# Routed attention with a squared-ReLU feed-forward on one core: the feed-forward of the last two batches by Strassen's algorithm after all attention, that of the first two spread evenly

## The chip, the cores and the metric

The kernel runs on one core of a Trainium2 chip. The metric is device time in microseconds (us) for one execution; the kernel before has a median of 1128.75 us over 3 runs (1128.17 to 1129.24). The profiler names the engines: PE (matrix products; PEld is its loading of the stationary operand), DVE (vector), ACT (scalar, activations), POOL (GpSimd), SP (issues the DMAs).

## What is computed

Four batches (b) of 768 tokens, eight heads of 64. Each query and key is assigned to the nearest of 16 centroids of its head; attention is masked to pairs of one cluster. The heads side by side form x (3072 x 512), which goes through a feed-forward:

```python
scores = scale * np.matmul(q, k.transpose(0, 1, 3, 2))
scores = np.where(mask, scores, -1000000000.0)
attn = softmax(scores)            # over keys
x = concat_heads(attn @ v)        # (3072, 512)
h = x @ w_in                      # w_in: 512 x 2048
g = np.maximum(h, 0) ** 2
out = g @ w_out                   # w_out: 2048 x 512
```

All of it is float32.

## The kernel before

**Attention.** Two heads (a pair) are worked on at once; there are 16 pairs, four for each batch. A pair has two query halves h of 384 tokens, and each half is done in three units, each over two chunks of 128 keys: 96 units. A unit on PE is a group of score products into `sc` (line 81 and 84, by `together`), ACT takes the exponential of 128x1536 (line 360), DVE multiplies by the mask in four instructions (line 366, from batch 1 on; batch 0 has its mask in the score products), POOL adds the exponentials up in `acc` (lines 376 and 378), and two units later PE multiplies by v into `av`. When a half of a pair is through, `finish` sums `acc` over the keys on PE (`sm`), DVE takes the reciprocal (line 416), scales `av` into the tile `xT` (line 417) and notes in `good` whether the numbers were in range (line 422).

**Feed-forward.** `ffn(b, h)` treats one half of a batch's tokens, 384 of them: 16 times four matmuls of 384 columns into `ph` (line 435), ReLU on ACT and squaring on DVE (`gT`, line 443); then for three blocks of 128 tokens 16 matmuls of 512 columns into `po` (line 448), an ACT copy and a DMA out. One half is 64 + 48 = 112 matmuls. A float32 matmul shows in the trace as two passes, each a MATMUL with a LDWEIGHTS of its own, so a half has 128 passes of 384 columns and 96 of 512.

**Order of the work.** `ffn` is a generator that yields after each matmul. The main loop over units calls `fill_steps` twice per unit, and so puts feed-forward matmuls between the attention products. Before the change the share per unit is what is left of the appended halves over the units until the next ones come: the two halves of batch b run beside the attention of batch b+1, and both halves of batch 3 run after all attention. Each engine works its own queue in order; the recording layer can move an instruction by priority, so the built order is shown below where it matters. After the last unit a check is made: `fine` sums `good` on DVE, PE adds it over the partitions (`every`, line 554), DVE makes `flag` (line 555). If it is set, `general_path` recomputes everything; it is not taken here.

**Weights** come in by DMA in the first 15 or so units and are rounded by ACT, DVE and POOL (lines 139 to 155).

Of the kernel before, what the change touches and what calls it, by code (L numbers as in the profile page):

```python
# [8 lines left out]
F32 = mybir.dt.float32  # L9
# [15 lines left out]
def kernel(  # L25
# [10 lines left out]
    nc = tc.nc  # L36

    B, H, S, D = q.shape
    C = centroids.shape[1]
    NCH = S // P  # L40
    DM = H * D
    DFF = moe_w_in.shape[1]
    KT = DM // P
    FT = DFF // P
    HP = H // 2
    NB = NCH // 2
    TB = NB * P
# [2 lines left out]
    SCALE = float(D) ** -0.5  # L50

    const = ctx.enter_context(tc.tile_pool(name="const", bufs=1))
    outer, ctx = ctx, ExitStack()
    loads = ctx.enter_context(tc.tile_pool(name="loads", bufs=4))
    loads_v = ctx.enter_context(tc.tile_pool(name="loads_v", bufs=2))
    qktp = ctx.enter_context(tc.tile_pool(name="qktp", bufs=HP))
# [3 lines left out]
    expp = ctx.enter_context(tc.tile_pool(name="expp", bufs=3))  # L60
    accp = ctx.enter_context(tc.tile_pool(name="accp", bufs=2))
    rbp = ctx.enter_context(tc.tile_pool(name="rbp", bufs=2))
    xtp = ctx.enter_context(tc.tile_pool(name="xtp", bufs=2))
    gtp = ctx.enter_context(tc.tile_pool(name="gtp", bufs=FT))

    early = ExitStack()
    wstage = early.enter_context(tc.tile_pool(name="wstage", bufs=AHEAD, side="right"))
    once_early = early.enter_context(tc.tile_pool(name="once_early", bufs=1, side="right"))
    later = {}
# [263 lines left out]
    def first_half(pair, h):  # L333
        return pair < HP and h == 0

    av = {}
    xT = {}
# [61 lines left out]
    def finish(pair, h):  # L399
        b, hp = divmod(pair, HP)  # L400
        if hp == 0:
            pool = xtp if (2 * b + h) % 3 < 2 else later["xT"]
            xT[b, h] = pool.tile([P, KT, TB], F32, name="xT")
        if first_half(pair, h):
            sm = sums.pop((pair, h))
        else:
            total = acc.pop((pair, h))
            sm = bank("sm", [P, TB])
            together(
                dict(  # L410
                    out=sm[D * e : D * (e + 1)], lhsT=ups, rhs=total[:, e], start=True, stop=True
                )
                for e in range(2)
            )
# [12 lines left out]

    out_view = out.rearrange("(b p j) m -> b j p m", p=P, j=NCH)

    def ffn(b, h):  # L430
        gT = []
        for f in range(FT):
            ph = bank("ph", [P, TB])
            for kk in range(KT):
                nc.tensor.matmul(  # L435
                    ph, lhsT=w_in[:, kk, f * P : (f + 1) * P], rhs=xT[b, h][:, kk],
                    start=(kk == 0), stop=(kk == KT - 1),
                )
                if kk < KT - 1:
                    yield  # L440
            gT.append(gtp.tile([P, TB], F32, name="gT"))
            nc.scalar.activation(out=gT[f], in_=ph, func=ACT.Relu)  # L442
            nc.vector.tensor_tensor(out=gT[f], in0=gT[f], in1=gT[f], op=ALU.mult)  # L443
            yield
        for i in range(NB):
            po = bank("po", [P, DM])
            for f in range(FT):
                nc.tensor.matmul(  # L448
                    po, lhsT=gT[f][:, i * P : (i + 1) * P], rhs=w_out[:, f],
                    start=(f == 0), stop=(f == FT - 1),  # L450
                )
                if f < FT - 1:
                    yield
            osb = later["out"].tile([P, DM], F32, name="osb")
            nc.scalar.copy(out=osb, in_=po)  # L455
            nc.sync.dma_start(out_view[b, h * NB + i], osb)
            yield

    units = [
        (pair, h, c)
        for pairs, halves in [(range(HP), [0]), (range(HP), [1])]
# [2 lines left out]
    ]  # L466
    LAG = 2
    per_half = FT * KT + NB * FT
    fill = []
    left = [0]  # L470

    def fill_steps(n):
        while n > 0 and fill:
            if next(fill[0], "end") == "end":
                fill.pop(0)
            else:
                n -= 1
                left[0] -= 1

    def next_pair(u):  # L480

        pair, h, c = units[u]
        if c == 0 and pair + 1 < NG and h == 0 and (pair + 1) not in qkT:
            if pair + 1 < HP or pair >= HP:
                return pair + 1
        if c == 0 and h == 1 and pair == HP - 1:
            return pair + 1
        return None
# [5 lines left out]
        item()  # L494
    load_v(0)
    ahead = []
    left_units = [0]
    for _ in range(AHEAD):
        load_weights(next(loaded))
    for u in range(len(units) + LAG):  # L500
        if u < len(units):
            pair, h, c = units[u]
            if (p := next_pair(u)) is not None:
                ahead.extend(prep(p))
            if c == 0 and u + 3 < len(units) and units[u + 3][0] not in raw_v:
                load_v(units[u + 3][0])
            scores(pair, h, c)
        done = None
        if u >= LAG:
            pair, h, c = units[u - LAG]  # L510
            times_v(pair, h, c)
            if c == NCH - 2:
                done = pair, h

        for _ in range(2):
            i = next(to_round, None)
            if i is not None:
                round_weights(i)
                if (i := next(loaded, None)) is not None:
                    load_weights(i)  # L520
            elif not later:
                early.close()
                for name, bufs in (("xT", 1), ("out", 2)):
                    later[name] = ctx.enter_context(
                        tc.tile_pool(name=name + "_late", bufs=bufs, side="right",
                                     reuse_waits="tile")
                    )
        share = -(-left[0] // max(1, left_units[0]))
        left_units[0] -= 1
        fill_steps(share // 2)  # L530
        for _ in range(3):
            if ahead:
                ahead.pop(0)()
        fill_steps(share - share // 2)
        if done:
            pair, h = done
            finish(pair, h)
            b, hp = divmod(pair, HP)
            if h == 1:
                for d in (qkT, ids, qid):  # L540
                    d.pop(pair)
            if h == 1 or b == 0:
                raw_v.pop(pair)
            if hp == HP - 1 and (h == 1 or b == 0):
                for hh in [h] if b == 0 else range(2):
                    fill.append(ffn(b, hh))
                    left[0] += per_half
                left_units[0] = NCH * HP // 2 if b == 0 and h == 0 else NCH * HP

    flag = const.tile([P, 1], I32, name="flag")  # L550
    fine = small.tile([P, 1], F32, name="fine")
# [3 lines left out]
    nc.vector.tensor_scalar(  # L555
        out=flag[0:1], in0=every, scalar1=UP * float(P * 2 * NG * TB), scalar2=None, op0=ALU.is_lt
    )
    for g in fill:
        for _ in g:
            pass  # L560

    ctx.close()
    again = nc.values_load(flag[0:1, 0:1], min_val=0, max_val=1)
    with tc.If(again != 0):
        general_path(
# [187 lines left out]
```

## Time and profile before

| | |
|---|---|
| median of 3 runs | 1128.75 us |
| profiled execution, its time | 1127.61 us |
| its span, first to last instruction | 1125.7 us |
| PE busy | 1084.8 us, 96% |
| DVE, POOL, ACT busy | 574.4, 318.6, 305.9 us |
| last attention product starts | 947.87 us |
| last feed-forward matmuls | 952.9 to 1119.9 us |

A matmul's end is modelled and overlaps the next one's start, so a pace is read from the distance between starts or from a long uninterrupted run, not from the length of one record.

### The profile page before, as it was taken

To read this page: it belongs to the slowest core of one execution; us is meant where nothing else is said; L and a number is where in the kernel's file an instruction comes from. 1 tells how busy PE (TensorE), PEld (TensorE's weight loads), DVE (VectorE), ACT (ScalarE), POOL (GpSimd) and SP (SyncE) were. 2 spreads that over 40 slices of the span, in tenths; PEclk is the share of its full clock that TensorE was granted. 3 is DMA by queue.
4 is the path that set the end of the run, shared out by engine and by line. 5 is a ranking of instruction groups with operands and counts; after the bars stand their busy time and mean duration, and the time that the engine had idled before them with its cause. 6 is when DMAs were issued, how large, how long until landed. Compare 5 with 4: busy or idle time off the path is not lost.

```text
span 1125.7 us, 10447 instructions
## 1 busy us (share of the span) xinstructions
PE 1084.8 (96%) x4195; PEld 503.9 (45%) x4195; DVE 574.4 (51%) x762; ACT 305.9 (27%) x416; POOL 318.6 (28%) x181
## 2 busy tenths in 40 slices
PE   5779999999999999999999999999999998999997
PEld 3333454444444344444445444444445443544543
DVE  4999222328886666672377544664466641200200
ACT  4666322223332223231232212231132210110100
POOL 2444433225443443331333222332232330000000
PEclk8899999999999999999999999999999999999999
DMA  8874000120110201010201002000000000000000
GB/s 226 224 236 152 15 15 14 52 61 1 43 43 1 52 10 52 1 43 9 52 10 42 1 9 61 1 15 10 10 24 0 1 10 19 1 10 19 1 10 21
DMA packets 63880, 44.30 MB, mean 39 GB/s; under 512 B 51536, under 2 KB 56656, under 8 KB 63824
## 3 DMA queue, kind: packets, MB, share of 16 engines
q1 hardware_dynamic: 63824, 43.56, 13.5%
q8 instruction: 35, 0.57, 0.2%
q14 instruction: 21, 0.17, 0.1%
HBM read 37.26 MB, written 6.29 MB: 39 GB/s over the span
## 4 chain that ended last, share of the span: by engine, by line
PE 86%; DVE 7%; issue 3%; DMA 1%; ACT 1%; POOL 1%; SPq 1%; ACTq 0%; POOLq 0%; DVEq 0%
PE po L448 30%; PE ph L435 29%; PE sc L81 6%; PE av L81 5%; PE sc L84 5%; PE av L84 5%; DVE ex L366 2%; PE sm L81 2%; PE pt L237 2%; DVE w_raw L151 1%; DMA w_raw<-in_moe_w_in_dram 1%; DVE rb L416 1%; PE lg L81 1%; PE pb L315 1%; POOL w_out L155 1%
## 5 line engine op out<-in xcount | busy, mean ns | idle before, releaser
L435 PE MATMUL ph<-xT,w_in 128*128 128x384 f32 x1024 | 352.7, 495 | 0.1
L448 PE MATMUL po<-w_out,gT 128*128 128x512 f32 x768 | 347.3, 599 | 0.0
L378 POOL TENSOR_TENSOR acc<-acc,ex 128x768 f32<-128x768 f32 x112 | 219.5, 1959 | 416.8 <-DVE ex L366 358.7
L366 DVE SCALAR_TENSOR_TENSOR ex<-qid,ids,ex 128x384 f32<-128x384 bf16 x288 | 246.2, 916 | 154.9 <-ACT ex L360 151.8
L435 PEld LDWEIGHTS ph<-xT,w_in 128*128 128x128 f32 x1024 | 188.6, 190 | 152.8 <-issue 33.4
L448 PEld LDWEIGHTS po<-w_out,gT 128*128 128x128 f32 x768 | 139.9, 190 | 173.1 <-issue 170.6
L360 ACT ACTIVATE ex<-sc 128x1536 f32<-128x1536 f32 x96 | 139.2, 1450 | 231.8 <-PE sc L84 231.8
L443 DVE TENSOR_TENSOR gT<-gT 128x384 f32<-128x384 f32 x128 | 95.5, 751 | 194.6 <-ACT gT L442 194.2
L84 PE MATMUL sc<-qkT 64*128 64x384 f32 x576 | 151.8, 506 | 0.0
L84 PE MATMUL av<-ex,v_raw 128*64 128x384 f32 x576 | 147.7, 498 | 0.0
L442 ACT ACTIVATE gT<-ph 128x384 f32<-128x384 f32 x128 | 62.9, 492 | 260.9 <-PE ph L435 260.9
L416 DVE RECIPROCAL rb<-sm 128x384 f32<-128x384 f32 x32 | 81.7, 2553 | 67.2 <-PE sm L84 67.1
L81 PE MATMUL sc<-qkT 64*128 64x384 f32 x192 | 89.2, 545 | 1.7 <-ACT ex L360 1.5
L376 POOL TENSOR_TENSOR acc<-ex 128x768 f32<-128x768 f32 x28 | 52.7, 1881 | 123.7 <-DVE ex L366 103.0
L81 PE MATMUL av<-ex,v_raw 128*64 128x384 f32 x192 | 83.1, 515 | 0.0
L84 PEld LDWEIGHTS sc<-qkT 64*128 64x128 f32 x576 | 66.7, 190 | 26.2 <-issue 2.1
L84 PEld LDWEIGHTS av<-ex,v_raw 128*64 128x64 f32 x576 | 46.6, 137 | 35.4 <-issue 35.1
L455 ACT COPY osb<-po 128x512 f32<-128x512 f32 x24 | 14.1, 586 | 175.7 <-PE po L448 175.7
L81 PEld LDWEIGHTS sc<-qkT 64*128 64x128 f32 x192 | 29.0, 189 | 50.3 <-issue 40.0
L81 PEld LDWEIGHTS av<-ex,v_raw 128*64 128x64 f32 x192 | 18.6, 135 | 44.0 <-issue 43.1
L151 DVE SCALAR_TENSOR_TENSOR w_raw<-w_raw 128x512 uint32<-128x512 uint32 x32 | 36.2, 1130 | 0.1
L155 POOL TENSOR_TENSOR w_in<-w_in,w_raw 128x512 int32<-128x512 int32 x16 | 21.7, 1358 | 43.6 <-DVE w_raw L151 38.5
(80 smaller groups left out, 500.8 us busy)
## 6 DMA issues: line engine op xcount, KB each, us to landing
w_raw<-in_moe_w_in_dram SPq DMA_DIRECT2D x16, 512.0 KB, 5.4
w_raw<-in_moe_w_out_dram SPq DMA_DIRECT2D x16, 512.0 KB, 3.5
v_raw<-in_v_dram SPq DMA_DIRECT2D x20, 384.0 KB, 3.3
q_raw<-in_q_dram SPq DMA_DIRECT2D x32, 192.0 KB, 3.5
k_raw<-in_k_dram SPq DMA_DIRECT2D x32, 192.0 KB, 3.9
out_dram<-osb SPq DMA_DIRECT2D x24, 256.0 KB, 2.0
cen<-in_centroids_dram SPq DMA_DIRECT2D x1, 32.0 KB, 1.8
```

The source lines that it names most:

```text
L81: nc.tensor.matmul(**next(products))
L84: nc.tensor.matmul(**product)
L151: nc.vector.scalar_tensor_tensor(out=lo, in0=hi, scalar=0x80000000, in1=lo, op0=ALU.bitwise_and, op1=ALU.bitwise_or)
L360: nc.scalar.activation(out=t, in_=sc.rearrange("p i e n -> p (i e) n")[:, :, 0:TB], func=ACT.Exp, scale=SCALE)
L366: nc.vector.scalar_tensor_tensor(out=to, in0=qid[pair][1][:, h, e], scalar=ids[pair][:, ch % NB, 2 + ch // NB, e : e + 1], in1=to, op0=ALU ...
L376: nc.gpsimd.tensor_tensor(out=acc[pair, h], in0=t[:, 0:2], in1=t[:, 2:4], op=ALU.add)
L378: nc.gpsimd.tensor_tensor(out=acc[pair, h], in0=acc[pair, h], in1=t[:, 2 * i : 2 * i + 2], op=ALU.add)
L416: nc.vector.reciprocal(out=rb, in_=sm)
L435: nc.tensor.matmul(ph, lhsT=w_in[:, kk, f * P : (f + 1) * P], rhs=xT[b, h][:, kk], start=(kk == 0), stop=(kk == KT - 1),)
L442: nc.scalar.activation(out=gT[f], in_=ph, func=ACT.Relu)
L443: nc.vector.tensor_tensor(out=gT[f], in0=gT[f], in1=gT[f], op=ALU.mult)
L448: nc.tensor.matmul(po, lhsT=gT[f][:, i * P : (i + 1) * P], rhs=w_out[:, f], start=(f == 0), stop=(f == FT - 1),)
```

## The change

The first two batches keep `ffn`: four halves (`PLAIN`), 448 matmuls, whose share per unit is now all that is left over all units that are left. Batches 2 and 3 are no longer filled in. When attention and the filling are done, `ctx.close()` gives its memory back and `ffn_pair` runs for batch 2 and then for batch 3, both halves of the batch at once.

`ffn_pair` multiplies by Strassen's algorithm in Winograd's form, one level: operands are cut into 2 x 2 blocks, seven products of blocks replace eight, and sums and differences of blocks are made before and after. First layer: x is cut by contraction (two of four 128-blocks) and by half h; w_in by contraction and by columns. For each of 8 pairs of column blocks there are 7 products of 2 matmuls of 384 columns. POOL makes four combinations of w_in blocks for each (`w_s1` to `w_s4`, 128x256), DVE four of x per batch (`x_t1`, `x_t2`, `x_t4`, and one in place, 128x768). Second layer: for each of 3 token blocks 7 products of 8 matmuls of 256 columns; POOL makes four combinations of w_out once (`w_t1` to `w_t4`, 128x2048), DVE four of g per token block (128x1024). `combine` takes the first product out of PSUM by an ACT copy and adds the others by seven DVE instructions. ReLU and squaring of one block in four are done by ACT, of the others by one DVE instruction each. The tile pool of PSUM banks has 8 buffers here.

```diff
-    outer, ctx = ctx, ExitStack()
+    outer, ctx, keep, early = ctx, ExitStack(), ExitStack(), ExitStack()
+    xtp = keep.enter_context(tc.tile_pool(name="xtp", bufs=2))
...
-            pool = xtp if (2 * b + h) % 3 < 2 else later["xT"]
+            pool = xtp if (2 * b + h) in (0, 1, 5, 6) else later["xT"]
...
+    def ffn_pair(pools, b):
+        gp, sp, tp, bk = pools
+        H2, F2, M2 = KT // 2, FT // 2, DM // 2
+        x = [[xT[b, h][:, H2 * g : H2 * (g + 1)] for h in range(2)] for g in range(2)]
+        t1, t2, t4 = (tp.tile([P, H2, TB], F32, name=f"x_t{i}") for i in (1, 2, 4))
...
+        sub(t1, x[0][1], x[0][0])
+        sub(t2, x[1][1], t1)
+        sub(t4, t2, x[1][0])
+        sub(x[0][1], x[1][1], x[0][1])
+        t3 = x[0][1]
+        g = gp.tile([P, FT, 2, TB], F32, name="g")
+        def combine(c, product, width):
+            (c11, c12), (c21, c22) = c
+            def add(j, *results):
+                bank = bk(width)
+                product(j, bank)
+                for out, to in results:
+                    nc.vector.tensor_tensor(out=out, in0=bank, in1=to, op=ALU.add)
+            bank = bk(width)
+            product(1, bank)
+            nc.scalar.copy(out=c11, in_=bank)
+            add(6, (c12, c11))
+            add(2, (c11, c11))
+            add(7, (c21, c12))
+            add(5, (c22, c21), (c12, c12))
+            bank = bk(width)
+            product(4, bank)
+            sub(c21, c21, bank)
+            add(3, (c12, c12))
+        for i in range(F2):
...
+            nc.gpsimd.tensor_tensor(out=s1, in0=a[1][0], in1=a[1][1], op=ALU.add)
+            sub(s2, s1, a[0][0], nc.gpsimd)
+            sub(s3, a[0][0], a[1][0], nc.gpsimd)
+            sub(s4, a[0][1], s2, nc.gpsimd)
+            operands = {
+                1: (a[0][0], x[0][0]), 2: (a[0][1], x[1][0]), 3: (s4, x[1][1]), 4: (a[1][1], t4),
+                5: (s1, t1), 6: (s2, t2), 7: (s3, t3),
+            }
...
+            combine(c, product, TB)
+            nc.scalar.activation(out=c[0][0], in_=c[0][0], func=ACT.Relu)
+            nc.scalar.square(c[0][0], c[0][0])
+            for to in (c[1][1], c[1][0], c[0][1]):
+                nc.vector.scalar_tensor_tensor(
+                    out=to, in0=to, scalar=0.0, in1=to, op0=ALU.max, op1=ALU.mult
+                )
+        for i in range(NB):
...
+            nc.vector.tensor_tensor(out=s1, in0=a[1][0], in1=a[1][1], op=ALU.add)
+            sub(s2, s1, a[0][0])
+            sub(a[1][0], a[0][0], a[1][0])
+            operands = {
+                1: (a[0][0], w_q[0][0]), 2: (a[0][1], w_q[1][0]), 3: (a[0][1], w_q[1][1]),
+                4: (a[1][1], w_t[4]), 5: (s1, w_t[1]), 6: (s2, w_t[2]), 7: (a[1][0], w_t[3]),
+            }
...
+            combine(c, product, M2)
+            for h in range(2):
+                nc.sync.dma_start(out_view[b, h * NB + i], osb[h])
...
+    PLAIN = [(0, 0), (0, 1), (1, 0), (1, 1)]
-    left = [0]
+    left = [len(PLAIN) * per_half]
...
-        share = -(-left[0] // max(1, left_units[0]))
+        share = -(-left[0] // (len(units) + LAG - u))
...
-    for g in fill:
-        for _ in g:
-            pass
+    fill_steps(left[0])
     ctx.close()
+    fast = ExitStack()
+    banks = fast.enter_context(tc.tile_pool(name="banks", bufs=8, space=PSUM))
...
+    for to, x, y in ((1, w_q[0][1], w_q[0][0]), (2, w_q[1][1], w_t[1]), (3, w_q[1][1], w_q[0][1]),
+                     (4, w_t[2], w_q[1][0])):
+        nc.gpsimd.tensor_tensor(out=w_t[to], in0=x, in1=y, op=ALU.subtract)
+    for b in range(B):
+        if (b, 0) not in PLAIN:
+            ffn_pair(pools, b)
```

Lines of the changed program are one higher than before up to the new functions.

PE's queue at the end of attention, before the change (`av`, `sm`: the last half of the last pair; `every`: the check):

```order
L448 MATMUL po<-w_out,gT 128x512 x9
L81 MATMUL av<-ex,v_raw 64x384
L84 MATMUL av<-ex,v_raw 64x384 x3
L448 MATMUL po<-w_out,gT 128x512 x9
L81 MATMUL sm<-acc,ups 64x384
L84 MATMUL sm<-acc,ups 64x384
L554 MATMUL every<-ups,fine 1x1
L435 MATMUL ph<-xT,w_in 128x384 x64
L448 MATMUL po<-w_out,gT 128x512 x48
```

The same place after the change (`bank`: a product of Strassen's algorithm; the numbers at `x_t` and `w_s` tell buffers apart, 4248 is `w_s2`, 4240 `x_t2`):

```order
L449 MATMUL po<-w_out,gT 128x512 x5
L82 MATMUL av<-ex,v_raw 64x384
L85 MATMUL av<-ex,v_raw 64x384 x3
L449 MATMUL po<-w_out,gT 128x512 x5
L82 MATMUL sm<-acc,ups 64x384
L85 MATMUL sm<-acc,ups 64x384
L650 MATMUL every<-ups,fine 1x1
L516 MATMUL bank<-xT,w_in 128x384 x2
L516 MATMUL bank<-x_t_4240,w_s_4248 128x384 x2
L516 MATMUL bank<-xT,w_in 128x384 x2
```

Between the last groups of `av` five matmuls of the filling stand in place of nine, and behind `every` PE meets as its second product one that needs a sum of POOL and a difference of DVE.

POOL's queue at that place, after the change (4231, 4233, 4232, 4234 are `w_t1`, `w_t3`, `w_t2`, `w_t4`; 4247 to 4250 are `w_s1` to `w_s4` of the first step). Before the change nothing but the check of `flag` follows the last `acc`:

```order
L379 TENSOR_TENSOR acc<-acc,ex 128x768 x4
L672 TENSOR_TENSOR w_t_4231<-w_out 128x2048
L672 TENSOR_TENSOR w_t_4233<-w_out 128x2048
L672 TENSOR_TENSOR w_t_4232<-w_out,w_t_4231 128x2048
L672 TENSOR_TENSOR w_t_4234<-w_t_4232,w_out 128x2048
L505 TENSOR_TENSOR w_s_4247<-w_in 128x256
L470 TENSOR_TENSOR w_s_4249<-w_in 128x256
L470 TENSOR_TENSOR w_s_4248<-w_s_4247,w_in 128x256
L470 TENSOR_TENSOR w_s_4250<-w_in,w_s_4248 128x256
```

The combinations of w_out, which only the second layer needs, stand ahead of those of w_in, which PE's second product needs. `w_t3` waits for the last `av` product, whose `v_raw` lay in its memory.

DVE's queue at the same place, after the change (`x_t1`, `x_t2`, `x_t4` of batch 2; the `xT` difference is the one in place):

```order
L470 TENSOR_TENSOR x_t1_4239<-xT_2683,xT_2535 128x768
L417 RECIPROCAL rb_4192<-sm_4189 128x384
L470 TENSOR_TENSOR x_t2_4240<-xT_2683,x_t1_4239 128x768
L418 SCALAR_TENSOR_TENSOR xT_3635<-av_4158,rb_4192 128x384
L423 SCALAR_TENSOR_TENSOR ok_4195,good_135<-rb_4192 128x384
L470 TENSOR_TENSOR x_t4_4241<-x_t2_4240,xT_2535 128x768
L648 TENSOR_REDUCE fine_4198<-good_135 128x1
L470 TENSOR_TENSOR xT_2683<-xT_2683 128x768
L651 TENSOR_SCALAR flag_4197<-every_4200 1x1
```

Before the change only the reciprocal, the scaling, `ok`, `fine` and `flag` stand there. The first product waits for `flag`, whose PSUM bank it takes over.

DVE's queue between the two layers of batch 2, after the change (4570 and 4574 are the banks of the last two products, `x_t*_48..` belong to batch 3, `g_s1` and `g_s2` to the second layer):

```order
L470 TENSOR_TENSOR g_4246<-g_4246,bank_4570 128x384
L470 TENSOR_TENSOR x_t1_4826<-xT_3635,xT_3493 128x768
L487 TENSOR_TENSOR g_4246<-bank_4574,g_4246 128x384
L526 SCALAR_TENSOR_TENSOR g_4246<-g_4246 128x384 x2
L470 TENSOR_TENSOR x_t2_4827<-xT_3635,x_t1_4826 128x768
L534 TENSOR_TENSOR g_s1_4583<-g_4246 128x1024
L470 TENSOR_TENSOR x_t4_4828<-x_t2_4827,xT_3493 128x768
L470 TENSOR_TENSOR g_s2_4584<-g_s1_4583,g_4246 128x1024
```

The second product of the second layer needs `g_s2`; three differences for batch 3 stand among the instructions that lead to it.

## Rows read from the trace of the kernel before

**Rows 1.** The page's first part: busy us, share of the span, instructions.

```profile
PE 1084.8 (96%) x4195; PEld 503.9 (45%) x4195; DVE 574.4 (51%) x762; ACT 305.9 (27%) x416; POOL 318.6 (28%) x181
```

**Rows 2.** Windows: stretch, us, busy (count) of each engine, granted clock, DMA.

```profile
111.00:947.80 836.80, 832.68 (x3278) 379.94 (x3276) 457.81 (x572) 219.47 (x282) 274.81 (x142) 1.00 0.08 22
947.80:952.90 5.10, 1.06 (x8) 0.33 (x7) 3.77 (x5) 0.59 (x1) 0.00 (x0) 1.00 0.14 51
952.90:1120.00 167.10, 166.91 (x450) 85.77 (x448) 18.02 (x33) 18.79 (x38) 0.00 (x0) 0.99 0.02 9
```

**Rows 3.** Chain that ended last, its tail: start, us, engine, tile, line, passes.

```profile
952.96 43.17 PE ph L435 x128
996.13 41.20 PE po L448 x96
1037.33 41.28 PE ph L435 x128
1078.61 41.21 PE po L448 x96
```

**Rows 4.** Timeline: one weight load among the 512-column passes; four transposes of 128 columns.

```profile
1118.36 0.19 PEld L448 LDWEIGHTS po<-w_out,gT 128*128 128x128 f32 x1 [0.24 <-issue]
...
741.94 0.42 PEld L237 LDWEIGHTS pt<-ident,q_raw 128*128 128x128 f32 x4 [0.55 <-ACT gT L442]
```

**Rows 5.** Windows of one stretch, of lines 435, 448 and 360 alone.

```profile
257.40:416.10 158.70, 44.13 (x122) 21.61 (x122) 1.00 0.10 26
...
257.40:416.10 158.70, 38.20 (x80) 13.90 (x80) 1.00 0.10 26
...
257.40:416.10 158.70, 30.48 (x21) 1.00 0.10 26
```

**Rows 6.** Timeline of the end of attention.

```profile
947.87 0.54 PE L81 MATMUL sm<-acc,ups 128*64 128x384 f32 x1
...
948.78 2.56 DVE L416 RECIPROCAL rb<-sm 128x384 f32<-128x384 f32 x1 [23.08 <-PE sm L84]
951.37 0.56 DVE L417 SCALAR_TENSOR_TENSOR xT<-av,rb 128x384 f32<-128x384 f32 x1
951.85 0.55 DVE L422 SCALAR_TENSOR_TENSOR ok<-rb 128x384 bf16<-128x384 f32 x1
...
952.77 0.19 PE L554 MATMUL every<-ups,fine 128*1 128x1 f32 x2 [4.04 <-DVE fine L552]
...
952.89 12.28 PE L435 MATMUL ph<-xT,w_in 128*128 128x384 f32 x32
```

**Rows 7.** Timeline of POOL and DVE side by side.

```profile
383.88 1.81 POOL L378 TENSOR_TENSOR acc<-acc,ex 128x768 f32<-128x768 f32 x1 [0.56 <-DVE ex L366]
...
384.51 0.56 DVE L272 TENSOR_TENSOR best<-lt,mx 128x384 bf16<-128x384 f32 x1
...
385.10 1.00 DVE L276 TENSOR_TENSOR best<-best,order 128x384 bf16<-128x384 bf16 x1
```

**Rows 8.** Lines 378 and 155: duration ns min/median/max, first and last start.

```profile
L378 POOL TENSOR_TENSOR acc<-acc,ex x112: 1802/2022/2211, 120.8 to 925.8; 128x768 f32<-128x768 f32 x112
...
L155 POOL TENSOR_TENSOR w_in<-w_in,w_raw x16: 1279/1304/1558, 16.7 to 66.9; 128x512 int32<-128x512 int32 x16
```

**Rows 9.** Timeline: two DVE instructions of 512 and 384 elements.

```profile
744.36 0.69 DVE L240 COPY qkT<-pt 128x512 f32<-128x512 f32 x1 [1.05 <-PE pt L237]
...
745.53 0.56 DVE L443 TENSOR_TENSOR gT<-gT 128x384 f32<-128x384 f32 x1 [0.48 <-ACT gT L442]
```

**Rows 10.** The page's fifth part: the mask multiply.

```profile
L366 DVE SCALAR_TENSOR_TENSOR ex<-qid,ids,ex 128x384 f32<-128x384 bf16 x288 | 246.2, 916 | 154.9 <-ACT ex L360 151.8
```

**Rows 11.** Timeline of the end of the span.

```profile
1119.89 0.59 ACT L455 COPY osb<-po 128x512 f32<-128x512 f32 x1 [13.15 <-PE po L448]
1120.50 0.33 SPq L456 DMA_DIRECT2D out_dram<-osb  x1
```

More of the change, by code (lines that the diff above doesn't have):

```diff
@@ L62 @@
     rbp = ctx.enter_context(tc.tile_pool(name="rbp", bufs=2))
-    xtp = ctx.enter_context(tc.tile_pool(name="xtp", bufs=2))
     gtp = ctx.enter_context(tc.tile_pool(name="gtp", bufs=FT))
-    early = ExitStack()
     wstage = early.enter_context(tc.tile_pool(name="wstage", bufs=AHEAD, side="right"))
@@ L457, in ffn, with sub, product @@
             yield
+    def ffn_pair(pools, b):
[3 more added lines that the diff above has]
+        t1, t2, t4 = (tp.tile([P, H2, TB], F32, name=f"x_t{i}") for i in (1, 2, 4))
+        def sub(out, a, b, eng=nc.vector):
+            eng.tensor_tensor(out=out, in0=a, in1=b, op=ALU.subtract)
+        sub(t1, x[0][1], x[0][0])
[23 more added lines that the diff above has]
+        for i in range(F2):
+            lo, hi = slice(i * P, (i + 1) * P), slice((F2 + i) * P, (F2 + i + 1) * P)
+            a = [[w_in[:, H2 * g2 : H2 * (g2 + 1), cols] for g2 in range(2)] for cols in (lo, hi)]
+            s1, s2, s3, s4 = (sp.tile([P, H2, P], F32, name=f"w_s{j}") for j in range(1, 5))
+            nc.gpsimd.tensor_tensor(out=s1, in0=a[1][0], in1=a[1][1], op=ALU.add)
[6 more added lines that the diff above has]
+            }
+            def product(j, bank):
+                for kk in range(H2):
+                    nc.tensor.matmul(
+                        bank, lhsT=operands[j][0][:, kk], rhs=operands[j][1][:, kk],
+                        start=(kk == 0), stop=(kk == H2 - 1),
+                    )
+            c = [[g[:, f, h] for h in range(2)] for f in (i, F2 + i)]
+            combine(c, product, TB)
[4 more added lines that the diff above has]
+                    out=to, in0=to, scalar=0.0, in1=to, op0=ALU.max, op1=ALU.mult
+                )
+        for i in range(NB):
+            cols = slice(i * P, (i + 1) * P)
+            a = [[g[:, F2 * g2 : F2 * (g2 + 1), h, cols] for g2 in range(2)] for h in range(2)]
+            s1, s2 = (sp.tile([P, F2, P], F32, name=f"g_s{j}") for j in (1, 2))
+            nc.vector.tensor_tensor(out=s1, in0=a[1][0], in1=a[1][1], op=ALU.add)
[5 more added lines that the diff above has]
+            }
+            def product(j, bank):
+                for f in range(F2):
+                    nc.tensor.matmul(
+                        bank, lhsT=operands[j][0][:, f], rhs=operands[j][1][:, f],
+                        start=(f == 0), stop=(f == F2 - 1),
+                    )
+                if j == 2:
+                    sub(a[0][1], a[0][1], s2)
+            osb = [later["out"].tile([P, DM], F32, name="osb") for _ in range(2)]
+            c = [[osb[h][:, M2 * m : M2 * (m + 1)] for m in range(2)] for h in range(2)]
+            combine(c, product, M2)
+            for h in range(2):
+                nc.sync.dma_start(out_view[b, h * NB + i], osb[h])
@@ L496 @@
     ahead = []
-    left_units = [0]
     for _ in range(AHEAD):
@@ L522 @@
                 early.close()
-                for name, bufs in (("xT", 1), ("out", 2)):
-                    later[name] = ctx.enter_context(
+                for name, bufs in (("xT", 3), ("out", 2)):
+                    later[name] = keep.enter_context(
                         tc.tile_pool(name=name + "_late", bufs=bufs, side="right",
@@ L527 @@
                     )
-        share = -(-left[0] // max(1, left_units[0]))
-        left_units[0] -= 1
+        share = -(-left[0] // (len(units) + LAG - u))
         fill_steps(share // 2)
@@ L544 @@
             if hp == HP - 1 and (h == 1 or b == 0):
[L545 to L548, printed above, removed]
+                for half in [(b, h)] if b == 0 else [(b, 0), (b, 1)]:
+                    if half in PLAIN:
+                        fill.append(ffn(*half))
     flag = const.tile([P, 1], I32, name="flag")
@@ L557 @@
     )
-    for g in fill:
-        for _ in g:
-            pass
+    fill_steps(left[0])
     ctx.close()
+    fast = ExitStack()
+    banks = fast.enter_context(tc.tile_pool(name="banks", bufs=8, space=PSUM))
+    wtp = fast.enter_context(tc.tile_pool(name="wtp", bufs=1, reuse_waits="tile"))
+    pools = [
+        fast.enter_context(tc.tile_pool(name=name, bufs=1, reuse_waits="tile"))
+        for name in ("gp", "sp", "tp")
+    ] + [lambda width: banks.tile([P, width], F32, name="bank", tag="bank")]
+    w_q = [
+        [w_out[:, FT // 2 * g : FT // 2 * (g + 1), DM // 2 * m : DM // 2 * (m + 1)] for m in range(2)]
+        for g in range(2)
+    ]
+    w_t = {i: wtp.tile([P, FT // 2, DM // 2], F32, name=f"w_t{i}") for i in range(1, 5)}
+    for to, x, y in ((1, w_q[0][1], w_q[0][0]), (2, w_q[1][1], w_t[1]), (3, w_q[1][1], w_q[0][1]),
[4 more added lines that the diff above has]
+            ffn_pair(pools, b)
+    fast.close()
+    keep.close()
     again = nc.values_load(flag[0:1, 0:1], min_val=0, max_val=1)
```

## Prediction

> **What bounds the kernel now.** I read the page's busy line first: PE is busy 96% of the span, every other engine about half or less [rows 1]. An average hides stages, so next the windows. From 111 us to the end of attention PE is busy 832.7 of 836.8 us at granted clock 1.00; then comes a hole of 5 us, and 167 us of feed-forward alone in which PE is again full and POOL idle [rows 2]. So PE sets the end nearly everywhere, and a matmul pass taken away is worth its own pace. The tail of the chain gives that pace without any modelled ends: 128 passes of 384 columns take 41.28 us, 0.3225 each, and 96 passes of 512 columns 41.21 us, 0.4293 each [rows 3]. The first run of 384 columns, behind the hole, took 1.9 us more; the mean clock of that stretch is 0.99. What the hole consists of I read from the timeline: from `sm` at 947.87 DVE needs the reciprocal, scaling, `ok` and `fine` before PE may do `every`, and `ph` starts at 952.89 [rows 6].
>
> **Products saved.** A batch now has 256 passes of 384 and 192 of 512 columns: 82.6 + 82.4 = 165.0 us. Strassen's form has 8 x 7 x 2 matmuls of 384 columns (224 passes) and 3 x 7 x 8 of 256 (336 passes). The trace has no weight-changing float32 pass of 256 columns. Between 384 and 512 the pace is 0.83 ns per column with 2 ns left over, so 256 columns should take 0.2157. Against that stands the weight load, recorded at 0.19 us for each pass [rows 4]: it fits under 0.2157, by little. Four loads of the same size for transposes took 0.42 us together, so they follow each other at 0.105 or less; I take 0.2157. The upper end would be pass and load one after the other, 0.213 + 0.19 = 0.40. With 0.2157: 72.2 + 72.5 = 144.7 us, 20.3 saved for a batch, **40.5 us** for two.
>
> **Attention with less filling.** Two of the six halves that were filled in leave it, 165 us, so `sm` should come at about 783. That holds if a unit still costs the same without its filling. Over 111 to 947.8 it is (836.8 - 495)/85 units = 4.02 us. The stretch with the thinnest filling, 202 passes over 21 units or 4.8 matmuls per unit, gives 158.7 - 122 x 0.3225 - 80 x 0.4293 = 85.0 us, 4.05 per unit [rows 5]. The change puts in 448/85 = 5.3. So the score, exponential, mask, product chain stays hidden; 0.03 us over some 70 units would be 2 us, I add **1**, with 0 and 4 as ends.
>
> **The hand-over.** Here the change adds waits. POOL's new queue has four 2048-element instructions ahead of the first `w_s`. The cheapest 512 and 768 elements took 1.28 and 1.80 us [rows 8], 2.04 ns per element, so 2048 should take 4.4 and 256 should take 0.76; at the median of 768 it would be 5.4. On DVE 384 and 512 elements take 0.56 and 0.69 [rows 9], so 768 take 0.95 and 1024 take 1.21. And the two engines hold each other up: while POOL added from 383.88 to 385.69, a DVE instruction with one operand in PSUM took its 0.56, the next one, with both in SBUF, took 1.00 and ended 0.4 behind POOL [rows 7]. The differences `x_t`, `ok` and the in-place one have both operands in SBUF.
>
> Take `sm` as zero. Between the last scores and `sm` PE has 15 matmuls of 512 columns (12.9 us) and four attention groups, some 20 us; POOL's last addition comes some 10 us after those scores (the exponential, 30.48/21 = 1.45 [rows 5], a reciprocal's work ahead of four masks at 0.92 [rows 10], additions of 2.0). So POOL starts `w_t1` at -10, `w_t3` behind the last `av` at -5, `w_t2` ends at 4.1. DVE does the reciprocal until 3.5, `x_t2` is held until 4.1 and ends at 5.1; `w_t4` runs from there to 9.5, the scaling beside it, `ok` is held until it ends: 10.0. `x_t4` takes turns with `w_s1` to 11.7; `fine` and `every` to 12.3; the in-place difference and `flag`, for which the first product waits, to about 13.7. `w_s2` is ready by then. Before, the same way took 5.0 [rows 6]: **+8.7**. Lower end: if nothing were held, POOL's queue alone ends `w_s2` at 10.7, against 6.3 for the second product before: +4.4. Upper end, POOL at 5.4 us: +13. The slow first microseconds of PE exist before as well; I leave them at nothing, up to 1.5 more.
>
> **Inside the Strassen stage.** A step of the first layer is 14 matmuls, 9.03 us. DVE has ten instructions of 0.56 in it, of which only the three squarings can be held, POOL four of 0.76: even one after the other 8.6. `w_s1` and `w_s2` of the next step may start when the fifth product is through, three products (3.9 us) ahead of their use, and need 2.6 with a DVE instruction before each. Eight banks let PE run ahead. So steps cost nothing beyond PE. Between the layers they do: behind the last product DVE has `x_t1`'s rest, an addition, two squarings, `x_t2`, `g_s1`, `x_t4`, `g_s2`, ending at 6.3; PE's next product, 8 matmuls of 0.431, covers 3.45. Wait 2.9 in batch 2. In batch 3 without the `x_t` the chain is 4.1, wait 0.7. Together **+3.6**, ends 0 (rearranged under another wait) and 7. Later blocks have `g_s2` queued ahead of the last products' additions. At the end an addition of 256 elements (0.43) stands for the copy of 0.59 before the last DMA [rows 11]: -0.2.
>
> **Sum.** 1125.7 - 40.5 + 1 + 8.7 + 3.6 - 0.2 = 1098.3 of span. The profiled execution took 1.9 more than its span (1127.6), and the median is 1.1 above it: **1101 us**, 2.4% less than 1128.75. Its own range from the ends above: 1092 to 1114.
>
> **Rivals.** Each has to eat 27 us to turn the sign.
>
> *Ports decide the first layer (ends slower).* POOL and DVE shut each other out [rows 7]; if a 256-element POOL instruction costs what one of 512 does (1.30 [rows 8]) and they strictly take turns, a step is 5.6 + 4 x 1.30 = 10.8 against 9.03, 16 steps lose 28: 1129. From 10.75 us per step on it decides; a little more and it is slower. For it: such holds are common in the trace. Against: seven of the ten DVE instructions of a step read PSUM, and the two POOL sizes have a clear slope. Chance 0.06.
>
> *Weight loads become the pace of 256 columns (ends slower).* 336 x 2 passes; each 0.041 us above 0.2157 is enough, that is 0.257 per pass. Pass and load in series gives 672 x 0.19 = +126: 1227. Against: loads at 0.105 [rows 4] and a pace of 0.4293 for 512 columns, of which a load in series would leave no trace. Chance 0.04.
> The Trainium skill ("TensorE: Matmul & The Clock Gate", Part 3, The mechanism) says that a weight load overlaps a running matmul only where the two use different row groups; here all 128 rows are used by both, so by that rule this rival would be certain. The trace disagrees: by the rule a 512-column pass would pace at no less than 0.43 + 0.19 = 0.62, and it paces at 0.4293 [rows 3].
>
> *Thin filling exposes the attention chain.* If units from batch 2 on cost 0.2 us more, +14: 1115. It would need 0.39 per unit to lose all. Against: [rows 5]. Chance 0.08.
>
> *No holding at the hand-over, boundaries hidden.* +4.4 and 0 instead of 8.7 and 3.6: 1093. For it: DVE may slip in between POOL's instructions in a better order. Chance 0.07.
>
> **Numbers.** The forecast itself 0.75. Predicted 1101; the range that leaves out some 2 in 10 is 1093 to 1115, which takes in the ends of the hand-over, the thin filling and the fast case. Faster by over 0.2% (what this kernel's spread of 0.1% lets one tell from nothing): 0.75 + 0.08 + 0.07 = 0.90. Within 0.2%: 0.02, from the port rival's edge. Slower: 0.08, the rest of that rival and the loads.
>
> **What will show it.** `sm` of the last pair at 783 +- 4; four POOL instructions of 4.4 to 5.4 us, the first about 10 us ahead of it; the first Strassen product 12 to 16 us behind it; steps of 9.0 us in the first layer; products of 8 matmuls 3.45 us apart in the second, 16 passes of 0.2157; a hole of about 3 us between the layers of batch 2 and under 1.5 in batch 3; PE's busy time down by some 40. A pace of 0.24 or more at 256 columns, steps above 9.5 us, or a hand-over above 20 us would make the forecast wrong, each for its own reason.

## The result, and the profile after

The changed kernel takes 1102.3 us (median of 4 runs, 1102.0 to 1105.7) against 1128.58 of the kernel before on the same chip (median of 4): a ratio of 0.9773, 95% interval [0.9754, 0.9793]. The prediction was 1101 us, range 1093 to 1115. The profiled execution took 1102.0, its span is 1099.9.

The engines' busy line of the page after, for the one in [rows 1]:

```profile
PE 1045.8 (95%) x4419; PEld 547.7 (50%) x4419; DVE 682.9 (62%) x932; ACT 293.2 (27%) x394; POOL 385.9 (35%) x249
```

PE has 39.0 us less to do, and DVE has 108.5 us more, beside it. The windows by stage, for [rows 2]: attention, hand-over, then first and second layer of batch 2 and of batch 3 (columns: stretch, length; busy us and count of PE, PEld, DVE, ACT, POOL; granted clock; DMA share; GB/s):

```profile
111.00:785.60 674.60, 670.09 (x2844) 296.47 (x2840) 440.40 (x544) 201.12 (x246) 281.73 (x145) 1.00 0.10 25
785.60:798.80 13.20, 1.09 (x8) 0.33 (x7) 12.20 (x9) 0.59 (x1) 13.12 (x6) 0.62 0.05 20
798.80:875.50 76.70, 76.70 (x236) 45.85 (x237) 46.62 (x82) 12.20 (x24) 26.65 (x34) 0.98 0.00 1
875.50:948.80 73.30, 70.42 (x326) 61.68 (x326) 24.31 (x35) 1.12 (x3) 0.00 (x0) 1.00 0.05 18
948.80:1024.80 76.00, 75.67 (x240) 45.23 (x239) 48.26 (x84) 12.49 (x25) 22.19 (x28) 1.00 0.01 4
1024.80:1094.30 69.50, 69.33 (x320) 60.72 (x320) 19.63 (x31) 0.83 (x3) 0.00 (x0) 1.00 0.06 20
```

PE is full in every stage but two: the hand-over, with 1.09 us of PE in 13.20, and the change of layer in batch 2 (70.42 of 73.30). The chain that ended last, for [rows 3] (start, length, what):

```profile
879.45 69.33 PE bank L544 x320
948.78 72.25 PE bank L516 x224
...
1024.85 69.35 PE bank L544 x320
1094.20 0.02 issue
1094.22 0.42 DVE osb L487
```

224 passes of 384 columns take 72.25 us, 0.3225 each as before; 320 of 256 columns 69.33, 0.2167 each. That is the pace on which the saving rests. The hand-over itself, from the timeline of PE, DVE and POOL, for [rows 6] (start, length, engine, line, operation, out<-in, shapes, count; in brackets the engine's idle time before it and what ended that):

```profile
775.67 4.52 POOL L672 TENSOR_TENSOR w_t<-w_out 128x2048 f32<-128x2048 f32 x1
...
785.62 0.54 PE L82 MATMUL sm<-acc,ups 128*64 128x384 f32 x1
...
785.79 4.50 POOL L672 TENSOR_TENSOR w_t<-w_out,w_t 128x2048 f32<-128x2048 f32 x1
...
786.53 2.56 DVE L417 RECIPROCAL rb<-sm 128x384 f32<-128x384 f32 x1 [5.53 <-PE sm L85]
789.01 2.10 DVE L470 TENSOR_TENSOR x_t<-xT,x_t 128x768 f32<-128x768 f32 x1
790.37 5.09 POOL L672 TENSOR_TENSOR w_t<-w_t,w_out 128x2048 f32<-128x2048 f32 x1
791.03 0.55 DVE L418 SCALAR_TENSOR_TENSOR xT<-av,rb 128x384 f32<-128x384 f32 x1
791.50 4.38 DVE L423 SCALAR_TENSOR_TENSOR ok<-rb 128x384 bf16<-128x384 f32 x1
...
797.51 0.19 PE L650 MATMUL every<-ups,fine 128*1 128x1 f32 x2 [11.03 <-DVE fine L648]
797.82 1.43 POOL L470 TENSOR_TENSOR w_s<-w_s,w_in 128x256 f32<-128x256 f32 x1
798.59 0.14 DVE L651 TENSOR_SCALAR flag<-every 1x1 int32<-1x1 f32 x1
798.78 2.93 PE L516 MATMUL bank<-xT,w_in 128*128 128x384 f32 x4 [1.08 <-DVE flag L651]
```

`ok` lasts 4.38 us beside `w_t4` and ends 0.4 us behind it; `xT`, which reads `av` from PSUM, runs beside the same POOL instruction in its 0.55. The first product comes 13.16 us behind `sm`.

### The profile page after: what moved, and what is told of

Its sections match the earlier page's. It is cut to its first block, busy times and chain, and to the rows that moved or that the text cites. A ratio compares the mean times of both kernels' runs of the same rounds, so it can differ in the third digit from the quotient of the medians.

```text
span 1099.9 us, 11222 instructions
## 1 busy us (share of the span) xinstructions
PE 1045.8 (95%) x4419; PEld 547.7 (50%) x4419; DVE 682.9 (62%) x932; ACT 293.2 (27%) x394; POOL 385.9 (35%) x249
## 3 DMA queue, kind: packets, MB, share of 16 engines
q1 hardware_dynamic: 63824, 43.56, 13.7%
## 5 line engine op out<-in xcount | busy, mean ns | idle before, releaser
L436 PE MATMUL ph<-xT,w_in 128*128 128x384 f32 x512 | 184.4, 499 | 0.1
L449 PE MATMUL po<-w_out,gT 128*128 128x512 f32 x384 | 181.6, 606 | 0.0
L436 PEld LDWEIGHTS ph<-xT,w_in 128*128 128x128 f32 x512 | 91.1, 189 | 83.5 <-issue 33.7
L449 PEld LDWEIGHTS po<-w_out,gT 128*128 128x128 f32 x384 | 67.4, 189 | 87.4 <-issue 86.6
L444 DVE TENSOR_TENSOR gT<-gT 128x384 f32<-128x384 f32 x64 | 59.7, 942 | 58.0 <-ACT gT L443 57.8
L487 DVE TENSOR_TENSOR g<-bank,g 128x384 f32<-128x384 f32 x96 | 51.9, 555 | 56.7 <-PE bank L516 56.7
L85 PEld LDWEIGHTS sc<-qkT 64*128 64x128 f32 x576 | 66.9, 190 | 26.4 <-issue 2.4
L544 PE MATMUL bank<-w_out,g 128*128 128x256 f32 x288 | 64.4, 379 | 0.0
L443 ACT ACTIVATE gT<-ph 128x384 f32<-128x384 f32 x64 | 31.4, 491 | 113.9 <-PE ph L436 113.8
L544 PEld LDWEIGHTS bank<-w_out,g 128*128 128x128 f32 x288 | 54.7, 190 | 7.9
```

The source lines that it names most:

```text
L436: nc.tensor.matmul(ph, lhsT=w_in[:, kk, f * P : (f + 1) * P], rhs=xT[b, h][:, kk], start=(kk == 0), stop=(kk == KT - 1),)
L449: nc.tensor.matmul(po, lhsT=gT[f][:, i * P : (i + 1) * P], rhs=w_out[:, f], start=(f == 0), stop=(f == FT - 1),)
L487: nc.vector.tensor_tensor(out=out, in0=bank, in1=to, op=ALU.add)
L544: nc.tensor.matmul(bank, lhsT=operands[j][0][:, f], rhs=operands[j][1][:, f], start=(f == 0), stop=(f == F2 - 1),)
```

## The experiments

Medians come from different chips, so kernels are compared by their ratio to the kernel before. Three distances in the traces are sharper than the medians; they are counted to the first `sm` row of the last pair:

| kernel | median us | ratio, 95% | unit 12's exponential to `sm` | `sm` to first product | `sm` to last addition |
|---|---|---|---|---|---|
| changed kernel | 1102.3 | 0.9773 [0.9754, 0.9793] | 668.30 | 13.16 | 308.60 |
| e2_wt_late | 1097.9 | 0.9734 [0.9714, 0.9754] | 668.30 | 7.60 | 304.29 |
| e3_check_late | 1103.7 | 0.9772 [0.9755, 0.9788] | 668.32 | 6.10 | 310.78 |
| e9_noroom | 1093.6 | 0.9684 [0.9668, 0.9701] | 668.29 | 4.89 | 301.71 |
| e4_both | 1092.7 | 0.9674 [0.9658, 0.9690] | 672.15 | 0.80 | 296.34 |
| e8_xt_late | 1089.3 | 0.9647 [0.9628, 0.9667] | 672.36 | 0.80 | 292.77 |
| e11_xt_place | 1084.8 | 0.9608 [0.9595, 0.9622] | 668.32 | 0.80 | 292.76 |

**e1_plain: only the moving.**

```diff
-    for b in range(B):
-        if (b, 0) not in PLAIN:
-            ffn_pair(pools, b)
+    for b in (2, 3):
+        for h in range(2):
+            for _ in ffn(b, h):
+                pass
```

> Only the moving, without Strassen: the feed-forward of batches 2 and 3 by the plain steps behind all attention, with the changed kernel's even filling of batches 0 and 1. Theory (the time comes from the 320 products that are not formed; the moving itself gives nothing): the saved 40.5 us are gone, and of the changed kernel's own costs only the thin filling is left (0 to +4), so within 1 us below to 4 us above the kernel before: 1128 to 1133 us, the matmul busy time back at some 1085 us. Rival (spreading the filling evenly, or the undisturbed tail, pays by itself): under 1125 us.

Measured: 1130.0 us, ratio 1.0005 [0.9995, 1.0014]; PE's busy time is back:

```profile
PE 1085.8 (96%) x4195; PEld 505.4 (45%) x4195; DVE 571.4 (51%) x762; ACT 304.4 (27%) x416; POOL 315.4 (28%) x181
```

(The 320 in the expectation is a slip: what is saved is the work of 32 matmuls of 384 columns and of 24 of 512.) The theory holds: spreading the filling and emptying the tail neither gave nor cost more than 1.6 us. All of the gain is products that are not formed.

**e2_wt_late: the subtractions of w_out out of the hand-over.**

```diff
-    for to, x, y in ((1, w_q[0][1], w_q[0][0]), (2, w_q[1][1], w_t[1]), (3, w_q[1][1], w_q[0][1]),
...
-        nc.gpsimd.tensor_tensor(out=w_t[to], in0=x, in1=y, op=ALU.subtract)
...
+            if i > 0:
+                next_w_t()
```

`next_w_t` issues one of the four subtractions behind the `w_s` of each of steps 1 to 4.

> The four 4.5 us subtractions of output weights on GpSimd are taken out of the hand-over: one each stands behind GpSimd's sums of steps 1 to 4 of batch 2's first layer. Theory (GpSimd's queue and its holds of VectorE set the hand-over): the first product starts 8 to 9 us behind the last score product instead of 13.2, and the time falls by 4 to 5 us, to 1097 to 1098.5. Rival (the check chain of normalisation, sum over keys and flag alone sets it, the subtractions lie beside it): the first product stays at 13 us and the time within 1 us of 1102.

Measured: ratio 0.9734 against 0.9773, some 4.4 us less. The two intervals just touch, but the tail shows the same, 4.3 us shorter. The theory holds, and the first product comes even a little earlier than it said, at 7.60. In the timeline of this kernel neither `x_t2` (0.89 us) nor `ok` is held any more; only the in-place difference and two `w_s` still take turns (1.38, 1.31 and 1.43 us):

```profile
787.91 0.55 DVE L423 SCALAR_TENSOR_TENSOR ok<-rb 128x384 bf16<-128x384 f32 x1
...
790.65 0.14 DVE L653 TENSOR_SCALAR flag<-every 1x1 int32<-1x1 f32 x1
...
790.85 2.92 PE L516 MATMUL bank<-xT,w_in 128*128 128x384 f32 x4 [1.08 <-DVE flag L653]
```

POOL's four instructions are the larger part of the hand-over's price: 5.6 of the 8.1 us by which the changed kernel's 13.16 exceeds the 5.02 of [rows 6]. The first product is 5.6 us earlier and the tail only 4.3 shorter: behind the change of layer in batch 2 the clock was 0.81 for 9 us here, and the stretch of 320 passes took 71.02 instead of 69.33.

**e3_check_late: the check out of the hand-over.** `fine`, `every` and `flag` are written behind batch 2's `ffn_pair`; nothing else changes.

> Only the check of the softmax sums (sum over keys, its product and the flag) is moved behind batch 2's feed-forward; the four subtractions on GpSimd stay first. Theory (GpSimd's queue is the limit that stands behind the check): the first product starts some 6 us behind the last score product, but the second waits for the weights' sum at 12 us, so the time falls by 2 to 4.5 us, to 1097.5 to 1100. Rival (the check chain is the only limit): 7 to 9 us less, 1093 to 1095. If it were the subtractions alone: no change.

Measured: ratio 0.9772, no change. Theory and rival both named a gain and both were wrong; the outcome is that of the third case. The first product is 7 us earlier, as expected, and gives it all back:

```profile
792.16 2.90 PE L516 MATMUL bank<-xT,w_in 128*128 128x384 f32 x4 [5.23 <-DVE xT L418]
795.87 1.03 POOL L505 TENSOR_TENSOR w_s<-w_in 128x256 f32<-128x256 f32 x1
...
799.75 2.93 PE L516 MATMUL bank<-x_t,w_s 128*128 128x384 f32 x4 [4.70 <-POOL w_s L470]
...
802.48 2.76 PE L516 MATMUL bank<-xT,w_in 128*128 128x384 f32 x4
```

The second product waits for `w_s2` behind POOL's four instructions, until 13.7 us behind `sm`, and the second and third still take 2.7 and 2.6 us from start to start instead of 1.29. In the changed kernel the second product starts at 15.9, so 2.2 us of the lead are left there; but the granted clock is 0.51 from 798.5 to 805.4 here, and by the start of the second layer, 87.5 us behind `sm` against 87.3, nothing is left. The tail is even 2.2 us longer; 1.7 of that are the 320 passes of batch 2's second layer, which took 71.02 as in e2_wt_late. So in the changed kernel two chains end within 1 us of each other, `w_s2` at 799.25 and `flag` at 798.73. Taking the check away leaves POOL's; taking POOL's four instructions away, as in e2_wt_late, also frees the check, since they are what holds `ok`.

**e4_both and e9_noroom: both moved, with and without early room.** e9_noroom is e2_wt_late and e3_check_late together. e4_both also lets the sums of x take room that comes free before attention ends, and lets each bank wait for its own last reader:

```diff
-    banks = fast.enter_context(tc.tile_pool(name="banks", bufs=8, space=PSUM))
+    banks = fast.enter_context(tc.tile_pool(name="banks", bufs=8, space=PSUM, reuse_waits="tile"))
-    wtp = fast.enter_context(tc.tile_pool(name="wtp", bufs=1, reuse_waits="tile"))
...
-        for name in ("gp", "sp", "tp")
...
+    tp, sp, wtp, gp = (
...
+        for name in ("tp", "sp", "wtp", "gp")
```

> Both moves at once, and the operands of the first Strassen products given room that is free early (their buffers are laid out in another order, and each bank waits for its own last reader). Theory (the 13.2 us between the last score product and the first Strassen product, and the low clock behind them, are all hand-over): the first product starts within 2 us of the last score product, the clock does not drop, and the time falls by 11 to 14 us, to 1088 to 1091. Rival (the softmax's tail on VectorE and ScalarE, which must run in any case, still holds the first steps' sums): 5 to 8 us less, 1094 to 1097.

> e4_both without its third part: subtractions and check late, but buffers and banks laid out as in the changed kernel. Theory (the room matters: the banks of the first product are free only when the last normalised output xT has been read from them, 4 to 5 us behind the last score product, and x's sums stand behind the reciprocal): the first product starts 4 to 5 us behind the last score product instead of 0.4, so about 7 us less than the changed kernel, 0.971 of the kernel before, some 1096 us. Rival (the order alone did it, the room is incidental): as e4_both, 0.967, 1092 us.

Measured: e4_both 0.9674, 11.2 us less than the changed kernel; the first product stands 0.80 us behind `sm` and the clock stays up there. That is as its theory said, but the time stands just above the theory's 1088 to 1091. Order of the pools and waits of the banks were changed together, and no run parts them. e9_noroom has its first product at 4.89, waiting for `xT` as expected, and a tail 6.9 us shorter:

```profile
790.41 2.90 PE L516 MATMUL bank<-xT,w_in 128*128 128x384 f32 x4 [4.02 <-DVE xT L418]
```

By the median it gains more than the expected 0.971, namely 0.9684, and the intervals of the two overlap, so the medians do not part them; the tails, 301.71 and 296.34, do. And e4_both gives part of it back where I had not looked: its attention takes 3.85 us longer. The place, in its timeline:

```profile
694.44 2.56 DVE L470 TENSOR_TENSOR xT<-xT 128x768 f32<-128x768 f32 x1
...
697.39 0.95 DVE L470 TENSOR_TENSOR x_t<-x_t,xT 128x768 f32<-128x768 f32 x1
698.26 0.54 DVE L271 TENSOR_REDUCE mx<-lt 128x24 f32<-128x384 f32 x1
...
700.95 0.17 DVE L292 CAST ids_b<-ids 128x12 bf16<-128x12 f32 x1
...
701.18 0.82 PE L316 MATMUL pb<-ident_b,ids_b 128*128 128x128 bf16 x6 [2.74 <-DVE ids_b L292]
701.93 0.90 PE L82 MATMUL av<-ex,v_raw 128*64 128x384 f32 x1
```

With room free early, batch 2's sums of x run as soon as that batch's attention is done, which is just where DVE forms the last pair's cluster indices; the one in place is also held beside a POOL addition, 2.56 us instead of 0.95. PE waits 2.74 us for them instead of 0.35, and the `av` products behind take 0.90 instead of 0.54.

**e8_xt_late: batch 3's sums of x behind the sums of g of batch 2's second token block.**

```diff
+            if i == 1 and b + 1 < B:
+                prepared[b + 1] = prepare(b + 1, True)
```

`prepare` forms `x_t1`, `x_t2`, `x_t4` and the difference in place.

> As e4_both, and batch 3's sums of x (four of 0.95 us on VectorE) stand behind the sums of g of batch 2's second layer instead of between them. Theory (these sums are what makes the first 256-column product of batch 2 wait 2.9 us, batch 3's only 0.4): the wait falls to 0.4 to 1 us, the time by 2 to 2.5 us against e4_both: 0.965 of the kernel before, 1089 to 1091. Rival (the chain of squares and g's sums alone is the wait): no change against e4_both, 0.9674.

Measured: 0.9647, as the theory said; its interval overlaps e4_both's, but the tail is 3.6 us shorter. The first 256-column product behind the change of layer:

```profile
866.02 3.72 PE L557 MATMUL bank<-w_t,g_s 128*128 128x256 f32 x16 [0.76 <-DVE g_s L470]
```

The wait is 0.76 instead of 2.86, and the clock stays up behind it, which is the other 1.5 us (the stretch of 320 passes took 70.81 in e4_both, 69.33 here).

**e11_xt_place: batch 2's sums of x where no indices are formed.**

```diff
+            with tc.issue_after(done_ok[0].ins):
+                prepared[b] = prepare(b, False)
```

`done_ok[0]` is the third last `ok`.

> As e8_xt_late, with the first Strassen batch's four sums of x placed: behind the third last normalisation of the attention, where no indices are being formed, instead of wherever their room comes free. Theory (in e4_both and e8_xt_late these sums stood on VectorE in the middle of the last pair's index chain, so TensorE waited 2.7 us for ids_b instead of 0.35 and ran at the lower clock behind it: exp of unit 12 to the last score product took 672.5 us instead of 668.7): that stretch is 668.7 again and the time 3 to 4 us under e8_xt_late: 1085 to 1087, 0.961 to 0.963 of the kernel before. Rival (the 3.8 us have another cause in that layout): 672.5 again, 0.9647.

Measured: 1084.8 us, 0.9608; the attention takes 668.32 again, and `pb` waits 0.35. (In the expectation the distances run to the second pair of `sm` rows, 0.4 later.)

```profile
698.49 0.51 PE L316 MATMUL pb<-ident_b,ids_b 128*128 128x128 bf16 x6 [0.35 <-DVE ids_b L292]
```

This is the best version, 18.6 us under the changed kernel by the ratios; 15.8 us of that stand in the tail, hand-over and change of layer together, and the rest, 2.8, is no more than the stretch ahead of unit 12 varies.

**e6_128: are weight loads near their limit?** Each second-layer product is formed as two of 128 columns.

> Each second-layer product of 256 columns is formed as two of 128: per batch 672 passes of 128 columns in place of 336 of 256, each with its own weight load (0.19 us in the profile). Theory (passes are paced by their columns down to the pace of the load; the 256-column pass of 0.2167 us just clears it): the load becomes the pace, 0.19 us or a little more per pass instead of 0.109, so 2 x 672 x 0.08 = +109 us: about 1210. Rival (loads that stand behind other passes are free at any width): 1102 to 1106.

Measured, one run: 1107.1 us, just above the rival's 1102 to 1106. The chain in the second layer of batch 2, and the windows over that of batch 3:

```profile
878.12 73.36 PE bank L546 x640
```

```profile
1027.50:1099.30 71.80, 71.73 (x640) 71.54 (x640) 19.55 (x30) 0.94 (x3) 0.00 (x0) 1.00 0.06 20
```

My theory falls: 640 passes in 71.73 us are 0.112 each, with a load of 0.192 us recorded for every one. PEld is busy 71.54 of 71.80 us while the 640 loads add up to 123, so loads overlap each other, and a row's length is not a pace. The 256-column pass was never near a limit.
The Trainium skill ("TensorE: Matmul & The Clock Gate", Part 3, The mechanism) lists under what overlaps that a weight load does so only with a matmul of another row group, though the opening of the same section also lets a load into a background weight buffer run ahead. Here every load and pass uses all 128 rows, and the trace disagrees with the first of the two: one pass with its load takes 0.112 us, where the load's row alone is 0.192 long.

**e5_three, e7_three_hand, e10_three_even: a third batch by Strassen's algorithm.** Only batch 0 stays in `PLAIN`, and q and k load through two buffers instead of four to make room. e7 and e10 have e4_both's hand-over; e5 and e7 end the filling 8 units before attention ends, e10 spreads it over all:

```diff
-    loads = ctx.enter_context(tc.tile_pool(name="loads", bufs=4))
+    loads = ctx.enter_context(tc.tile_pool(name="loads", bufs=2))
...
-    PLAIN = [(0, 0), (0, 1), (1, 0), (1, 1)]
+    PLAIN = [(0, 0), (0, 1)]
...
-        share = -(-left[0] // (len(units) + LAG - u))
+        share = -(-left[0] // max(1, len(units) + LAG - u - 8))
```

The last change, of `share`, is in e5 and e7 alone.

> Three batches by Strassen instead of two: only batch 0's feed-forward fills the attention, batches 1 to 3 come behind it; the thin filling is then 2.6 products for each pair of heads' softmax unit. Theory (the attention's own chain stays hidden behind products at that filling): one more batch saves half of 40.5, so 20 less, plus 1 to 4 for one more layer boundary: 1083 to 1087. Rival (thin filling lays the attention's chain on VectorE open, 5.4 us busy of some 6 us per unit): half to all of the gain is lost, 1092 to 1105.

> Three batches by Strassen, with the hand-over of e4_both (subtractions and check late, room given early). Theory: 20 less than e4_both if the attention's chain stays hidden, 1071 to 1077. Rival (the attention's chain is laid open by the thin filling): no better than e4_both, 1085 to 1100.

> As e7_three_hand, with batch 0's feed-forward spread over all units instead of ending 8 units early. Theory (at 2.6 products per unit the attention's chain is open all the way; the bare last 8 units are only part of it): some 10 to 15 us better than e7_three_hand, 1098 to 1105, still above e8_xt_late. Rival (only the bare units cost): 38 us better, 1073 to 1080.

Measured: 1129.5 (1.001 [0.999, 1.003]), 1113.8 (0.9863) and 1100.7 us (0.9764): all worse than e4_both, although each saves another 20 us of products. In e10_three_even, what PE waited for between 123 and 785 us (total, times, longest; attention ends at 648 here, and the last two lines lie behind it):

```profile
PE pb L316 <- DVE ids_b L292: 18.5, 11, 2.9
PE bank L546 <- DVE g_s L470: 2.9, 1, 2.9
PE bank L516 <- DVE rb L417: 2.3, 1, 2.3
```

and in the changed kernel over the same time:

```profile
PE pb L316 <- DVE ids_b L292: 3.6, 7, 1.1
```

At 2.6 products per unit the chain that forms the cluster indices on DVE is no longer hidden; at 5.3 it is. From unit 12 to `sm` e10_three_even takes 524.8 us, where 668.3 less the 165 of a batch would be 503.3: 21.5 lost, the whole gain. PE is idle for 22.1 us of that stretch, against 4.3 in the changed kernel. In e7_three_hand the stretch takes 539.6, so the 8 bare units cost 14.8 more. For e5_three and e7_three_hand the theory fell, and both came out worse than even the rival's ranges. For e10_three_even the theory held: 13 us better than e7_three_hand, inside 1098 to 1105.

One thing in these three is not explained: the exponential of unit 12 starts at 119.7 to 122.9 us, where the kernels with four load buffers have 114.9 to 117.7. Of the 9.5 us by which e10_three_even's span exceeds e4_both's, 6.4 stand there. The two load buffers may be the cause; no run changes them alone.

## Why the prediction was right, step by step

- **Products saved (40.5).** Right. The new number in it, 0.2157 us for a pass of 256 columns, measured 0.2167, which is 0.7 us over 672 passes. PE's busy time fell by 39.0, and e1_plain, without the saved products, lost the whole gain.
- **Attention with less filling (+1).** Right as to cause. `sm` came at 785.62 instead of 783, but 2.2 of that stand ahead of unit 12, whose exponential started at 117.3 instead of 115.1, in the stretch of weight loading; from there to `sm` the time beside the filling is 339.6 us against 339.1 before, 4.04 per unit in both (668.30 less 508 passes of 384 and 384 of 512 columns; 832.73 less 764 and 576). That the stretch ahead varies from kernel to kernel without a change in its work (114.9 to 117.7 over e1 to e4) I had not allowed for; it is inside the range.
- **The hand-over (+8.7).** The first product came at 13.16, predicted 13.7, and link by link as argued from [rows 7, 8]: `w_t1` 9.95 us ahead of `sm`, subtractions of 4.50 to 5.09, `x_t2` and `ok` held by the POOL instruction beside them, ending 0.8 and 0.4 us behind it. By the Trainium skill ("GPSIMD Engine Reference", Key points) GpSimd contends with VectorE instructions that read two operands from SBUF; the trace agrees, with 4.38 us for `ok` against 0.55, and 0.55 for `xT` with one operand in PSUM. e2_wt_late shows that these holds and POOL's queue are the larger part of the price, e3_check_late that the check alone is not.
- **The slow start of PE behind the hand-over (left at nothing).** Right: from the first product to the second layer are 74.17 us, against 72.25 for the same work in batch 3, so 1.9 more, as before the change (43.17 against 41.28 in [rows 3]). The clock row stands at 0.50, its 1.2 GHz level, from 788.8 to 802.5, while PE waited and for its first products:

```profile
788.80:802.50 13.70, 3.90 (x8) 2.30 (x9) 9.93 (x9) 0.48 (x1) 11.10 (x6) 0.50 0.00 0
```

- **Steps of the first layer at no cost.** Right: 9.03 us each, products 1.29 apart, although the squarings were held (1.05 instead of 0.56 beside POOL). The rival of the ports is gone.
- **The change of layer (+3.6).** 2.88 and 0.38 against 2.9 and 0.7. e8_xt_late shows the cause that was named, batch 3's sums of x on DVE. It can cost more than the wait: behind it the clock fell in e2_wt_late, e3_check_late, e4_both and e6_128 and took another 1.5 to 1.7 us; in the changed kernel and in e9_noroom it did not.
- **Rivals.** Weight loads: not even at 128 columns (672 loads of 0.19 us would be 128 us, not the 126 of the prediction; nothing rests on it). Thin filling: not at 5.3 products per unit, but at 2.6, where it ate the 20 us of a further batch. No holding at the hand-over: `x_t2` and `ok` were held.
- **The sum.** It came out 1.6 us short of the span of 1099.9: `sm` 1.75 later than the 783.87 in it and the 256-column passes 0.7 longer, the hand-over 0.5 and the waits between layers 0.3 shorter. No large errors cancelled.

What the prediction did not see is that most of its own +8.7 and +3.6 was a matter of order: e11_xt_place has all the savings without them.

## What to carry to other kernels

When work is moved behind a stage that hides everything, the price is at the seam: look which engine's queue the new operands stand in, and put behind the seam what only later work needs. When two chains end together there, taking one away can show nothing, as in e3_check_late; move both. And an operand made early must be placed, not only allowed early: on an engine in order it delays whatever chain it lands in.

## What the runs showed that was not expected

- Float32 weight loads whose rows are 0.192 us long pass at one per 0.112 us: a row's length is 1.7 times the pace.
- A wait of PE of 2.9 us between two full stretches is sometimes followed by the lower clock and sometimes not (1.00 in the changed kernel); a wait of 0.76 us was not, in two kernels. The first 9 us behind it in e2_wt_late:

```profile
871.00:880.00 9.00, 8.93 (x34) 7.52 (x35) 2.48 (x5) 0.00 (x0) 0.00 (x0) 0.81 0.00 0
```

- From unit 12 to `sm` seven kernels (the five of the table, e1_plain and e6_128) repeat 668.29 to 668.32 us, over at least three chips, while the 115 us ahead of it, with its DMAs, vary by 2.8 us. A distance between two rows settled what medians with intervals of 0.3 to 0.4% could not.
